# A constant for TensorE's idle matmuls, and a load of w1 split around a table: a fused spectral filter and Mish layer on one core

## The chip, the cores and the metric

The kernel runs on one core of a Trainium2 chip. The metric is the device time of one execution in microseconds. Three runs of the kernel before gave 135.14, 135.55 and 136.71 us, median 135.55.

## The reference

For x of 2048 x 512 (bf16) the reference mixes two branches by a gate for each row:

```
g = sigmoid((x * gate_w).sum(-1, keepdims=True))
a = irfft2(rfft2(x) * (w_r + 1j * w_i))          # spectral branch
h = x @ w1 + b1                                  # w1: 512 x 1792
b = (h * tanh(softplus(h))) @ w2                 # Mish, w2: 1792 x 512
out = g * a + (1 - g) * b
```

## The kernel before, in words

x is held as 16 tiles of 128 rows, in four chunks of four tiles. The spectral branch does both transforms as matmuls: TensorE transposes each x tile (`tr`, L516), VectorE forms sums and differences of the transposed tiles (L541, into Tg), TensorE multiplies these with a table FD (`a1`, L609 to L612) and then with matrices M1 (`s1`, L630); the result goes through a scratch tensor in HBM, is multiplied by the filter WT, and comes back by the inverse steps (L745, L798, L828, L846). The dense branch is layer 1 (`mm1`, L575: 14 column blocks of w1 for each chunk), Mish on ScalarE (L560), and layer 2 (L903).

The order of the work is not written out by hand. `_build` adds tasks with an engine, an estimated duration, a priority and their dependences to a graph; `schedule` walks through simulated time and lists the tasks of each engine: at each step it takes, of the tasks that could start within 0.1 us of the earliest, the one of highest priority. A load's estimated landing is when its turn on the DMA engines comes, plus its bytes over the `bw` entered for it, plus 0.6 us; a reader on another engine is due 0.05 us later. `run_engine` (L940) then issues each engine's list in that order, with semaphore waits where a dependence asks for one. So entered costs decide the order and nothing else; on the chip an engine waits in its list until the next task's inputs are there.

What the change touches lies in the head, the first ten or so microseconds:

- SyncE's queue issues the loads in the order of the code: the first half of x's chunk 0 (`ld_x0(0)`), row block 0 of w1's first 512 columns (`ld_w1d(0)`), the second half of the chunk (`ld_x0(1)`), the row blocks 1 to 3, the columns 512 to 1023 of w1 (`ld_w1(4, 8)`, 512 KB), the table FD (`ld_fd`, 192 KB), then chunk 1 of x, the rest of w1 (`ld_w1(8, 14)`), M1, chunks 2 and 3 of x, and small tables.
- GpSimd's queue holds the loads of the filter (WT) and of w2, which wait for the rest of w1.
- VectorE sets a tile zt of 128 x 256 to zero (L500). ScalarE applies Mish to one column of it (L501), which makes it load its function table. TensorE multiplies zt by itself (L504, the "idle" or filler matmuls): their results are not used. The planner puts such matmuls wherever TensorE has nothing else ready, until the first group of layer 1 is placed; at most 60 are offered, the first 15 of 256 columns, the rest of 128.
- Then come the small transpose of b1 (`tr_small`, L519), the transposes of the first half of the chunk, the first quarter of layer 1's first four column blocks on that half (`early0`, L590, which needs row block 0), the transposes of the second half, `early1` to `early3` (row blocks 1 to 3), and `late0` to `late3` (L590 too), the same four column blocks on the second half. Column block 4 (L575) follows, and the first `a1`, which needs FD.

L416 is the helper that issues every DMA, and L1017 the start of the program, where the engines meet and GpSimd writes a few built-in constants of one column.

Of the kernel before, what the change touches and what calls it, by code (L numbers as in the profile page):

```python
# [7 lines left out]
BF = mybir.dt.bfloat16  # L8
F32 = mybir.dt.float32
AF = mybir.ActivationFunctionType  # L10
# [20 lines left out]
def _bf16_bits(a):  # L31
    a = np.ascontiguousarray(a, dtype=np.float32)
    u = a.view(np.uint32)
    r = (u + np.uint32(0x7FFF) + ((u >> np.uint32(16)) & np.uint32(1))) >> np.uint32(16)
    return r.astype(np.uint16)
# [280 lines left out]
def _build(nc, A_x, A_w_r, A_w_i, B_x, B_w1, B_b1, B_w2, gate_w, out):  # L316
    cs = _build_consts()
    d_FD = nc.inline_tensor(_bf16_bits(cs["FD"]), name="c_fd").bitcast(BF)
# [7 lines left out]
    G = _Graph()  # L326
    es = ExitStack()
    with es:
        def sb(name, shape, dt):
            return es.enter_context(nc.sbuf_tensor(name, shape, dt))  # L330

        xo = sb("xo", [128, NT, 512], BF)
# [4 lines left out]
        act = sb("act", [128, 3, NFT, 512], BF)  # L337
        w1_sb = sb("w1_sb", [128, 4, F], BF)
        w2_sb = sb("w2_sb", [128, NFT, 512], BF)
        FDs = sb("FDs", [128, 768], BF)  # L340
# [6 lines left out]
        Ybuf = sb("Ybuf", [128, 32 * KR], BF)  # L347
        junk = sb("junk", [128, 512], BF)
        gwb = sb("gwb", [128, 512], BF)
        zt = sb("zt", [128, 256], BF)  # L350
        braw = sb("braw", [14, 128], BF)
        b1f = sb("b1f", [128, NFT], F32)
        gdot = sb("gdot", [128, NT], F32)
# [12 lines left out]
        q1 = sb("q1", [128, 2, 2, 16], F32)  # L366
# [25 lines left out]
        ps = es.enter_context(nc.psum_tensor("ps", [128, 8, 512], F32))  # L392
        psb = ps.bitcast(BF)

        xv = A_x[0].rearrange("(s p b) d -> p s b d", s=2, b=8)
        ov = out[0].rearrange("(s p b) d -> p s b d", s=2, b=8)
        w1v = B_w1.rearrange("(dt p) f -> p dt f", p=128)
# [7 lines left out]
        def new_sem(name):  # L405
            return es.enter_context(nc.semaphore(name))
# [5 lines left out]
        def dma(name, dst, src, reads=(), writes=(), nbytes=0, deps=(), is_out=False, prio=None, queue="sp", bw=300e3):  # L412
            dur = 1.0 if queue == "pool" else 0.5

            def fn(e, _dst=dst, _src=src):
                return e.dma_start(_dst, _src)  # L416

            t = G.add(name, queue, dur, fn, reads=reads, writes=writes, lat=2.0 + nbytes / bw, deps=deps, prio=prio)
            t.xfer = nbytes / bw
            t.isdma = True  # L420
            if is_out:
                t.sem = out_sem
                n_out_dma[0] += 1
                t.semval = 16 * n_out_dma[0]
            else:
                t.sem = new_sem("d_" + name)
                t.semval = 16
            return t
# [16 lines left out]
        def evict(name, n, dst, src, reads, writes, prio=None, rate=1.0):  # L445
# [9 lines left out]
              reads=["ones"], writes=["perm"])  # L455
        G.add("id14", "pool", 0.2, lambda e: e.affine_select(out=id14[:, :], in_=id14[:, :], pattern=[[1, 14]],
                                                             compare_op=ALU.is_equal, fill=0.0, base=0, channel_multiplier=-1),
              reads=["ones"], writes=["id14"])

        def ld_x(c, s0, s1):  # L460
            dma(f"ld_x{c}{s0}", xo[:, 4 * c + 2 * s0:4 * c + 2 * s1, :].rearrange("p (s b) d -> p s b d", b=2), xv[:, s0:s1, 2 * c:2 * c + 2, :],
                writes=[("x", t) for t in range(4 * c + 2 * s0, 4 * c + 2 * s1)], nbytes=128 * 2048 * (s1 - s0), bw=330e3 if c == 1 else 380e3)

        def ld_x0(b):
            dma(f"ld_x0{b}", xo[:, b:4:2, :], xv[:, :, b, :], writes=[("x", b), ("x", 2 + b)], nbytes=128 * 2048, bw=(218e3, 350e3)[b])

        def ld_w1d(dt_):
            dma(f"ld_w1d{dt_}", w1_sb[:, dt_, 0:512], w1v[:, dt_, 0:512], writes=[("w1d", dt_)], nbytes=128 * 1024, bw=350e3)

        def ld_w1(lo, hi):  # L470
            return dma(f"ld_w1_{lo}", w1_sb[:, :, 128 * lo:128 * hi], w1v[:, :, 128 * lo:128 * hi],
                       writes=[("w1", f) for f in range(lo, hi)], nbytes=512 * 256 * (hi - lo), bw=220e3 if lo == 4 else 380e3)

        dma("ld_b1", braw[:, :], B_b1.rearrange("(ft p) -> ft p", p=128), writes=["braw"], nbytes=3584, queue="act", prio=100.0)
        ld_x0(0)
        ld_w1d(0)
        ld_x0(1)
        for dt_ in range(1, 4):
            ld_w1d(dt_)
        ld_w1(4, 8)  # L480
        dma("ld_fd", FDs[:], d_FD[:], writes=["FD"], nbytes=128 * 1536, bw=262e3)
        ld_x(1, 0, 2)
        t_w1 = ld_w1(8, 14)
        dma("ld_m1", m1g1[:, 0:2048], d_M1.rearrange("p b h c m -> p (b h c m)"), writes=["m1"], nbytes=128 * 4096)
        ld_x(2, 0, 2)
# [4 lines left out]
        for i in range(2):  # L490
            for q in (0, 2, 1, 3):
                dma(f"ld_W{i}{q}", WT[32 * q:32 * q + 32, i, :, :].rearrange("p g k -> p (g k)"), Wv[i][q],
                    writes=[("W", i, q)], nbytes=32 * 8224, queue="pool", deps=[t_w1])
        WALL = [("W", i, q) for i in range(2) for q in range(4)]
        for h in range(2):
            dma(f"ld_w2_{h}", w2_sb[:, 7 * h:7 * (h + 1), :], w2v[:, 7 * h:7 * (h + 1), :],
                writes=[("w2", h)], nbytes=128 * 7 * 1024, queue="pool", deps=[t_w1])


        G.add("zero", "dve", 0.15, lambda e: e.memset(zt[:, :], 0.0), writes=["zt"], prio=99.0)  # L500
        G.add("table", "act", 1.5, lambda e: e.activation(q1[:, 0, 0, 0:1], zt[:, 0:1], AF.Mish), reads=["zt"], prio=99.0)  # L501
        for i in range(NWARM):
            n_ = 256 if i < 15 else 128
            G.add(f"warm{i}", "pe", n_ / 1200, lambda e, n_=n_: e.matmul(ps[:, 6, 0:n_], zt[:, 0:128], zt[:, 0:n_], start=True, stop=True),  # L504
               reads=["zt"], prio=1.0).filler = True


        SP0 = PR['sp0']
# [2 lines left out]
        def f_tr(e, ts, dts, at):  # L511
# [8 lines left out]
           reads=["braw", "id14"], writes=[("bank", 0)], prio=SP0 + 4.0)  # L520
        G.add("ev_small", "act", 0.25, lambda e: e.activation(b1f[:, :], psb[:, 0, 0:14], AF.Copy), reads=[("bank", 0)], writes=["b1f"], prio=SP0 + 1.05)
        for b in range(2):
            for dt_ in range(4):
                bk = (dt_ + 1) % 4
                pe(f"tr{b}d{dt_}", 2 * mm((256, 128)[b]), lambda e, dt_=dt_, bk=bk, b=b: f_tr(e, (b, 2 + b), (dt_,), lambda t, d_: (bk, t // 2)),
                   reads=[("x", b), ("x", 2 + b), "perm"], writes=[("bank", bk)], prio=SP0 + 1.0 + 2.5 * b - 0.01 * dt_)
# [3 lines left out]
                      reads=[("bank", bk)], writes=[("xT", t, dt_) for t in (b, 2 + b)], prio=SP0 + 1.1)  # L530

        for c in range(NCH):
            for t in range(4 * c, 4 * c + 4):
                if c > 0:
                    pe(f"tr{t}", 4 * mm(128), lambda e, t=t: f_tr(e, (t,), range(4), lambda t, dt_: (1, dt_)), reads=[("x", t), "perm"],
                       writes=[("bank", 1)], prio=SP0 + 1.0)
# [7 lines left out]
            for h, op in ((0, ALU.add), (1, ALU.subtract)):  # L544
# [3 lines left out]
                lo, hi = uv[:, 0:2, r2, :], uv[:, 2:4, r2, :]  # L548
# [45 lines left out]
        for dt_ in range(4):  # L594
            t_e = pe(f"early{dt_}", 4 * mm(256) * (1.8 if dt_ == 0 else 1), lambda e, dt_=dt_: f_early(e, range(4), (dt_,), 0), writes=[("bank", b) for b in EB],
                     reads=[("xT", 0, dt_), ("xT", 2, dt_), ("w1d", dt_)], prio=PR['mm1c0'] + 8)
            if dt_ == 0:
                G.filled = t_e
        for ft in range(4):
            pe(f"late{ft}", 4 * mm(256), lambda e, ft=ft: f_early(e, (ft,), range(4), 1), writes=[("bank", EB[ft])],  # L600
               reads=[("xT", t, dt_) for t in (1, 3) for dt_ in range(4)] + [("w1d", dt_) for dt_ in range(4)], prio=PR['mm1c0'] + 7 - 0.01 * ft)
            mish(0, ft, EB[ft])

        for t in range(NT):
            a1b = t % 2 if t >= 8 else 0

            def f_a1(e, t=t, a1b=a1b):
# [9 lines left out]
               writes=[("bank", a1b)], prio=SP0)  # L617
# [4 lines left out]
            if t % 4 == 3:  # L622
# [17 lines left out]
                for h in range(2):  # L640
                    t_r1w.append(dma(f"r1w{t}_{h}", scr1_w[h][:, b0:b0 + 8, :], Y1[64 * h:64 * h + 64, b0:b0 + 8, :],
                                     reads=[("Y1", b0 + i) for i in range(8)], writes=[("scr1", b0 + i, h) for i in range(8)],
                                     nbytes=64 * 8 * 512, prio=SP0 + 1.0, bw=180e3))
# [3 lines left out]
        for t in range(NT):  # L647
# [3 lines left out]
                  reads=[("x", t), "gw"], writes=[("gd", t), "junk"], deps=s1_tasks[2:3])  # L651
# [37 lines left out]
        for n in range(4):  # L689
            t_r1r.append(dma(f"r1r{n}", In2[:, :, 2 * n:2 * n + 2, :].rearrange("p q u k -> p q (u k)"), scr1_r[:, :, 512 * n:512 * n + 512],  # L690
                             reads=[("scr1", b, h) for b in range(32) for h in range(2)],
                             writes=[("In2", q, u) for q in range(4) for u in (2 * n, 2 * n + 1)],
# [43 lines left out]
        for n in range(4):  # L736
            zb = n % 2

            def f_s2(e, n=n):
                ins = None  # L740
                for c in range(2):
                    for q in range(4):
                        for h in range(2):
# [6 lines left out]
                               reads=[("In2", q, 2 * n + uu) for q in range(4) for uu in range(2)] + ["sm"], writes=BSB))  # L750
            for i in range(4):
                h, uu = divmod(i, 2)
                u, pb = 2 * (2 * n + uu) + h, uu
                for (nm, Pb, Wu) in (("1", P1b, WT[:, :, u, 0:256]), ("2", P2b, WT[:, ::-1, u, 0:256])):
# [5 lines left out]
                          reads=[("bank", 2 * h), ("bank", 2 * h + 1)] + WALL, writes=[("P" + nm, pb)])  # L760
                for (c, nm, Pb, op) in ((0, "1", P1b, ALU.subtract), (1, "2", P2b, ALU.add)):
# [3 lines left out]
                                reads=[("P" + nm, pb)], writes=[("Z", zb, i, c)])  # L765
                if n == 0 and i == 1:
                    s2_tasks.append(pe("s2x", 0.8, f_s2x, reads=[("In2", q, u_) for q in range(4) for u_ in range(8)] + ["sm", "rr"],
                                       writes=[("bank", 0), ("bank", 1)]))
# [4 lines left out]
                          reads=["q"], writes=["zr"])  # L773
                    G.add("zi", "pool", 0.15, lambda e: e.tensor_tensor(out=zi[:], in0=q2[:, 0], in1=q2[:, 1], op=ALU.add),
                          reads=["q"], writes=["zi"])
                    G.add("z0r", "pool", 0.15, lambda e: e.tensor_tensor(out=z0[:, 0, :], in0=zr[:, 0, :], in1=zi[:, 1, :], op=ALU.subtract),
                          reads=["zr", "zi"], writes=["z0r"])
                    G.add("z0i", "pool", 0.15, lambda e: e.tensor_tensor(out=z0[:, 1, :], in0=zi[:, 0, :], in1=zr[:, 1, :], op=ALU.add),
                          reads=["zr", "zi"], writes=["z0i"])
            if n == 0:  # L780
                G.add("gexp", "pool", 2.9, lambda e: e.tensor_tensor(out=gexp[:, :], in0=gbase[:, :], in1=gdot[:, :], op=ALU.pow),  # L781
                      reads=[("gd", t) for t in range(NT)] + ["gbase"], writes=["gexp"])
                G.add("gden", "pool", 0.2, lambda e: e.tensor_scalar(out=gexp[:, :], in0=gexp[:, :], scalar1=1.0, scalar2=None, op0=ALU.add),
                      reads=["gexp"], writes=["gden"])
                G.add("gcol", "dve", 0.2, lambda e: e.reciprocal(out=gcol[:, :], in_=gexp[:, :]), reads=["gden"], writes=["gcol"])
                G.add("omg", "dve", 0.1, lambda e: e.tensor_scalar(out=omg[:, :], in0=gcol[:, :], scalar1=-1.0, scalar2=1.0, op0=ALU.mult, op1=ALU.add),
                      reads=["gcol"], writes=["omg"])
            G.add(f"wc_{n}", "pool", 0.2, lambda e, n=n, zb=zb: e.tensor_copy(
                out=Zb[:, zb, :, :, :, 0], in_=z0[:].rearrange("p c (u h) -> p h c u", h=2)[:, :, :, 2 * n:2 * n + 2]),
                reads=["z0r", "z0i"], writes=[("Z", zb, 4)])  # L790

            def f_s2i(e, zb=zb):
# [10 lines left out]
               writes=BSB)  # L803
# [3 lines left out]
            for h in range(2):  # L807
                t_r2w.append(dma(f"r2w{n}{h}", scr2_w[h][:, :, 512 * n:512 * n + 512],
                                 T2s[64 * h:64 * h + 64, :, 2 * n:2 * n + 2, :].rearrange("p q u k -> p q (u k)"),
                                 reads=[("T2s", n, 0), ("T2s", n, 1)], writes=[("scr2", n, h)], nbytes=64 * 4096))  # L810
# [3 lines left out]
        for tq in range(8):  # L814
            b0 = 4 * tq
            dma(f"r2r{tq}", T2r[:, b0:b0 + 4, :], scr2_r[:, b0:b0 + 4, :],
                reads=[("scr2", n, h) for n in range(4) for h in range(2)], writes=[("T2r", b0 + i) for i in range(4)],
# [49 lines left out]
        for c in range(NCH):  # L867
# [7 lines left out]
            for tl in range(4):  # L875
                t = 4 * c + tl
                bank = 4 + (t % 2)
                if t == NT - 1:
                    G.cur_prio = PR['mm2'] - 10
                    for i, (c0, w_) in enumerate(((0, 384), (384, 128))):  # L880
                        cs_, bk = slice(c0, c0 + w_), 1 + i

                        def f_mm2h(e, t=t, tl=tl, bk=bk, hb=hb, cs_=cs_, w_=w_):
                            ins = None
                            for ft in range(NFT):
# [5 lines left out]
                           writes=[("bank", bk)])  # L891
# [3 lines left out]
                              reads=[("bank", bk), "omg", ("ga", t, 0), ("ga", t, 1), ("x", t)], writes=[("o", t, i)], prio=PR['fin'])  # L895
# [3 lines left out]
                for lo, hi in ((0, 4), (4, 7), (7, 11), (11, 14)):  # L899
                    def f_mm2(e, t=t, tl=tl, bank=bank, lo=lo, hi=hi, hb=hb):  # L900
# [7 lines left out]
                       reads=[("act", hb, ft) for ft in range(lo, hi)] + [("w2", lo // 7)], writes=[("bank", bank)])  # L908
                if t < NBF:
                    evict_b(t, bank)  # L910
                else:
# [3 lines left out]
                          reads=[("bank", bank), "omg", ("ga", t, 0), ("ga", t, 1)], writes=[("x", t), ("o", t)], prio=PR['fin'])  # L915
# [75 lines left out]
def bass_gated_mix__spectral_gfnet__dense_activation_mish__prompt_kernel(  # L991
    nc: bass.Bass,
    A_x: bass.AP,
    A_w_r: bass.AP,
    A_w_i: bass.AP,
    B_x: bass.AP,
    B_w1: bass.AP,
    B_b1: bass.AP,
    B_w2: bass.AP,
    gate_w: bass.AP,  # L1000
    out: bass.AP,
):
    _build(nc, A_x, A_w_r, A_w_i, B_x, B_w1, B_b1, B_w2, gate_w, out)
# [28 lines left out]
```

## Time and profile before

| | us |
|---|---|
| median of three runs | 135.55 |
| lowest, highest | 135.14, 136.71 |
| the profiled execution | 135.63 |
| its span, from the first to the last instruction | 133.9 |

The page gives busy time by engine (PE is TensorE's matmuls, PEld its loads of stationary operands, DVE VectorE, ACT ScalarE, POOL GpSimd, SP SyncE). The chain that ended last follows the work back from the last instruction, at each step to what released it; cut to a window and put in order of time, it reads as a list of what the kernel's end hung on. A group's line gives shortest, median and longest duration; a matmul's duration includes the time that it spends in the pipeline, so the rate is read from how many start in a stretch. A load's line gives its size and the time from issue to landing.

### The profile page before, as it was taken

What the parts mean: (1) busy time and instruction counts of PE and PEld (TensorE: products, weight loads), DVE (VectorE), ACT (ScalarE), POOL (GpSimd) and SP (SyncE); (2) the same over time, 40 slices, a digit from 0 to 9 for tenths busy, and PEclk for the clock granted to TensorE, in tenths of its full rate; (3) what the DMA queues carried; (4) which work ended last, traced back from release to release, by engine and by line L of the source; (5) the groups of instructions that cost most, each with busy time, mean ns of one, the idle gap of its engine ahead of it and who ended that gap; (6) DMA issues with size and microseconds to landing.
All of it is one profiled execution on the core that took longest, in us unless ns stands there. A gap on an engine that the chain in (4) does not pass through costs nothing.

```text
span 133.9 us, 2695 instructions
## 1 busy us (share of the span) xinstructions
PE 128.9 (96%) x1030; PEld 69.5 (52%) x1047; DVE 88.9 (66%) x213; ACT 79.6 (59%) x130; POOL 27.4 (20%) x56
## 2 busy tenths in 40 slices
PE   6999999999999999999999999999999999999992
PEld 4885655655544443443443443443445877755452
DVE  0286298989689982963893893794001699999422
ACT  4258798899988786605256657434333789792000
POOL 2000793014000009583440440440000000000000
PEclk9999999999999999999999999999999999999999
DMA  3899999999262399450600600600649700305321
GB/s 114 238 294 367 397 284 299 288 366 344 62 157 58 99 293 334 98 220 0 157 5 0 157 2 0 156 6 0 157 150 277 204 2 0 130 32 215 113 102 42
DMA packets 18937, 20.82 MB, mean 155 GB/s; under 512 B 1196, under 2 KB 16172, under 8 KB 18540
## 3 DMA queue, kind: packets, MB, share of 16 engines
q1 hardware_dynamic: 17888, 16.67, 41.1%
q0 software_dynamic: 864, 3.94, 9.4%
q8 instruction: 8, 0.13, 0.4%
q10 hardware_dynamic: 172, 0.04, 0.1%
q14 instruction: 5, 0.04, 0.1%
HBM read 14.35 MB, written 6.29 MB: 154 GB/s over the span
## 4 chain that ended last, share of the span: by engine, by line
PE 90%; ACT 6%; issue 1%; DVE 0%
PE ps L903 34%; PE ps L575 31%; PE ps L846 5%; ACT act L560 3%; PE ps L828 3%; ACT Ybuf L447 3%; PE ps L504 2%; PE ps L516 2%; PE ps L886 2%; PE ps L612 2%; PE ps L590 2%; PE ps L798 2%; PE ps L745 2%; PE ps L630 1%; PE ps L609 1%
## 5 line engine op out<-in xcount | busy, mean ns | idle before, releaser
L575 PE MATMUL ps<-xT,w_sb 128*128 128x512 bf16 x199 | 48.1, 379 | 0.8 <-issue 0.2
L903 PE MATMUL ps<-w_sb,act 128*128 128x512 bf16 x202 | 46.9, 379 | 0.6 <-issue 0.3
L560 ACT ACTIVATE act<-ps,b1f 128x512 bf16<-128x512 f32 x56 | 37.8, 692 | 12.8 <-PE ps L575 10.9
L903 PEld LDWEIGHTS ps<-w_sb,act 128*128 128x128 bf16 x210 | 20.2, 98 | 23.2 <-issue 1.2
L575 PEld LDWEIGHTS ps<-xT,w_sb 128*128 128x128 bf16 x208 | 19.4, 98 | 22.3 <-issue 2.1
L756 DVE TENSOR_TENSOR misc<-ps,WT 128x512 f32<-128x512 f32 x32 | 19.8, 681 | 5.9 <-PE ps L745 5.9
L858 ACT ACTIVATE xo<-ps,omg 128x512 bf16<-128x512 f32 x12 | 8.3, 690 | 19.5 <-PE ps L903 18.9
L762 POOL TENSOR_TENSOR misc<-misc 128x255 bf16<-128x255 f32 x17 | 12.1, 732 | 18.4 <-DVE misc L756 18.4
L446 DVE CAST Ybuf<-ps 128x512 bf16<-128x512 f32 (+1 forms) x9 | 8.2, 926 | 9.1 <-PE ps L798 7.3
L850 ACT ACTIVATE misc<-ps,gcol 128x512 f32<-128x512 f32 x16 | 10.7, 692 | 2.5 <-PE ps L846 2.4
L853 DVE TENSOR_TENSOR Tg<-misc 128x256 bf16<-128x256 f32 x32 | 11.7, 419 | 0.6 <-ACT misc L850 0.5
L446 DVE CAST misc<-ps 128x512 bf16<-128x512 f32 x7 | 4.8, 687 | 10.5 <-PE ps L828 10.5
L447 ACT ACTIVATE Ybuf<-ps 128x512 bf16<-128x512 f32 (+1 forms) x15 | 9.9, 714 | 2.9 <-PE ps L798 2.8
L649 DVE SCALAR_TENSOR_TENSOR junk<-xo,gwb 128x512 bf16<-128x512 bf16 x16 | 11.0, 690 | 0.7
L846 PE MATMUL ps<-GDs,misc 128*128 128x256 bf16 x64 | 9.3, 273 | 0.0
L447 ACT ACTIVATE Abuf<-ps 128x512 bf16<-128x512 f32 x13 | 7.7, 604 | 0.0
L446 DVE COPY xT<-ps 128x512 bf16<-128x512 bf16 x10 | 4.2, 422 | 4.6 <-PE ps L516 4.5
L516 PEld LDWEIGHTS ps<-pid,xo 128*128 128x128 bf16 x64 | 5.6, 111 | 3.1 <-DVE xT L446 0.4
L846 PEld LDWEIGHTS ps<-GDs,misc 128*128 128x128 bf16 x64 | 6.0, 98 | 2.1
L516 PE MATMUL ps<-pid,xo 128*128 128x128 bf16 x64 | 6.8, 243 | 0.0
L781 POOL TENSOR_TENSOR gexp<-gbase,gdot 128x16 f32<-128x16 f32 x1 | 2.9, 2943 | 18.5 <-DVE junk L649 18.5
L612 PE MATMUL ps<-FDs,Tg 128*128 128x256 bf16 x32 | 6.0, 273 | 0.0
(85 smaller groups left out, 112.8 us busy)
## 6 DMA issues: line engine op xcount, KB each, us to landing
scr<-Ybuf SPq DMA_DIRECT2D x16, 256.0 KB, 3.9
Abuf<-scr SPq DMA_DIRECT2D x4, 512.0 KB, 5.8
Abuf<-scr SPq DMA_DIRECT2D x8, 256.0 KB, 4.9
w_sb<-in_B_w_dram POOLq DMA_DIRECT2D x2, 896.0 KB, 14.2
out_dram<-xo SPq DMA_DIRECT2D x7, 256.0 KB, 2.1
xo<-in_A_x_dram SPq DMA_DIRECT2D x3, 512.0 KB, 9.8
WT<-in_A_w_r_dram POOLq DMA_DIRECT2D x4, 257.0 KB, 9.1
WT<-in_A_w_i_dram POOLq DMA_DIRECT2D x4, 257.0 KB, 10.8
```

The costliest lines, as they stand in the source:

```text
L446: G.add_multi(name, [("dve", dve_dur(n, rate=rate), lambda e: e.tensor_copy(out=dst, in_=src)), ("act", act_dur(n), lambda e: e.activation ...
L447: ("act", act_dur(n), lambda e: e.activation(dst, src, AF.Copy))],
L516: ins = e.transpose(psb[:, bank, 128 * col:128 * col + 128], xo[:, t, 128 * dt_:128 * (dt_ + 1)], perm[:, :])
L560: lambda e: e.activation(act[:, c % 3, ft, :].rearrange("p (t a b) -> p t a b", t=4, b=4), ps[:, bank, :].rearrange("p (t b a) -> p t a b" ...
L575: ins = e.matmul(ps[:, bank, :], w1_sb[:, dt_, 128 * ft:128 * (ft + 1)], xT[:, dt_, 4 * c:4 * c + 4, :], start=(dt_ == 0), stop=(dt_ == 3))
L649: lambda e, t=t: e.scalar_tensor_tensor(out=junk[:, :], in0=xo[:, t, :], scalar=1.0, in1=gwb[:, :], op0=ALU.mult, op1=ALU.mult, accum_out= ...
L756: lambda e, Pb=Pb, Wu=Wu, h=h, uu=uu, pb=pb: e.tensor_tensor(out=Pb[:, pb, :].rearrange("p (c j m) -> p c j m", c=2, j=2), in0=ps[:, 2 * h ...
L762: fz = (lambda e, c=c, Pb=Pb, op=op, pb=pb, h=h, uu=uu, zb=zb: e.tensor_tensor(out=Zb[:, zb, h, c, uu, 1:256], in0=Pb[:, pb, 1:256], in1=P ...
L846: ins = e.matmul(ps[:, yk, 256 * (j // 2):256 * (j // 2) + 256], TT[:, ts_, j // 2, s1, j % 2, :], GDs[:, j, :], start=(j % 2 == 0), stop= ...
L850: G.add(f"geo_{t}", "act", act_dur(512, True), lambda e: e.activation(gEO[:, gb, :], ps[:, yk, :], AF.Copy, scale=gcol[:, t:t + 1]), reads ...
L853: fg = (lambda e, i=i, op=op: e.tensor_tensor(out=ga[:, t, 256 * i:256 * i + 256], in0=gEO[:, gb, 0:256], in1=gEO[:, gb, 256:512], op=op))
L903: ins = e.matmul(ps[:, bank, :], act[:, hb, ft, 128 * tl:128 * (tl + 1)], w2_sb[:, ft, :], start=(ft == 0), stop=(ft == NFT - 1))
```

## The change

The idle matmuls read a built-in constant 1.0 of the library, one column wide and repeated by its access pattern, instead of the tile zt. The tile, its memset and the dependences on it go; the table's Mish reads the constant too. The first eight idle matmuls have 128 columns, the others 64, and the planner is told n / 600 us for n columns where it was told n / 1200. The load of w1's columns 512 to 1023 becomes two of 256 columns each, and the load of FD stands between them. The entered bandwidths of the head's loads change.

```diff
-        zt = sb("zt", [128, 256], BF)
...
         def ld_x0(b):
-            dma(f"ld_x0{b}", ..., nbytes=128 * 2048, bw=(218e3, 350e3)[b])
+            dma(f"ld_x0{b}", ..., nbytes=128 * 2048, bw=(403e3, 262e3)[b])
 
         def ld_w1d(dt_):
-            dma(f"ld_w1d{dt_}", ..., nbytes=128 * 1024, bw=350e3)
+            dma(f"ld_w1d{dt_}", ..., nbytes=128 * 1024, bw=(187e3, 238e3, 291e3, 187e3)[dt_])
 
         def ld_w1(lo, hi):
             return dma(f"ld_w1_{lo}", w1_sb[:, :, 128 * lo:128 * hi], w1v[:, :, 128 * lo:128 * hi],
-                       ..., bw=220e3 if lo == 4 else 380e3)
+                       ..., bw={4: 194e3, 6: 291e3}.get(lo, 380e3))
...
-        ld_w1(4, 8)
-        dma("ld_fd", FDs[:], d_FD[:], writes=["FD"], nbytes=128 * 1536, bw=262e3)
+        ld_w1(4, 6)
+        dma("ld_fd", FDs[:], d_FD[:], writes=["FD"], nbytes=128 * 1536, bw=115e3)
+        ld_w1(6, 8)
         ld_x(1, 0, 2)
...
-        G.add("zero", "dve", 0.15, lambda e: e.memset(zt[:, :], 0.0), writes=["zt"], prio=99.0)
-        G.add("table", "act", 1.5, lambda e: e.activation(q1[:, 0, 0, 0:1], zt[:, 0:1], AF.Mish), reads=["zt"], prio=99.0)
+        ones = nc.const_aps.tensor(1.0, (128, 256))
+        G.add("table", "act", 1.5, lambda e: e.activation(q1[:, 0, 0, 0:1], ones[:, 0:1], AF.Mish), prio=99.0)
         for i in range(NWARM):
-            n_ = 256 if i < 15 else 128
-            G.add(f"warm{i}", "pe", n_ / 1200, lambda e, n_=n_: e.matmul(ps[:, 6, 0:n_], zt[:, 0:128], zt[:, 0:n_], start=True, stop=True),
-               reads=["zt"], prio=1.0).filler = True
+            n_ = 128 if i < 8 else 64
+            G.add(f"warm{i}", "pe", n_ / 600, lambda e, n_=n_: e.matmul(ps[:, 6, 0:n_], ones[:, 0:128], ones[:, 0:n_], start=True, stop=True),
+                  prio=1.0).filler = True
```

More of the change, by code (lines that the diff above doesn't have):

```diff
@@ L464, in ld_x0 @@
         def ld_x0(b):
-            dma(f"ld_x0{b}", xo[:, b:4:2, :], xv[:, :, b, :], writes=[("x", b), ("x", 2 + b)], nbytes=128 * 2048, bw=(218e3, 350e3)[b])
+            dma(f"ld_x0{b}", xo[:, b:4:2, :], xv[:, :, b, :], writes=[("x", b), ("x", 2 + b)], nbytes=128 * 2048, bw=(403e3, 262e3)[b])
         def ld_w1d(dt_):
-            dma(f"ld_w1d{dt_}", w1_sb[:, dt_, 0:512], w1v[:, dt_, 0:512], writes=[("w1d", dt_)], nbytes=128 * 1024, bw=350e3)
+            dma(f"ld_w1d{dt_}", w1_sb[:, dt_, 0:512], w1v[:, dt_, 0:512], writes=[("w1d", dt_)], nbytes=128 * 1024, bw=(187e3, 238e3, 291e3, 187e3)[dt_])
         def ld_w1(lo, hi):
             return dma(f"ld_w1_{lo}", w1_sb[:, :, 128 * lo:128 * hi], w1v[:, :, 128 * lo:128 * hi],
-                       writes=[("w1", f) for f in range(lo, hi)], nbytes=512 * 256 * (hi - lo), bw=220e3 if lo == 4 else 380e3)
+                       writes=[("w1", f) for f in range(lo, hi)], nbytes=512 * 256 * (hi - lo), bw={4: 194e3, 6: 291e3}.get(lo, 380e3))
         dma("ld_b1", braw[:, :], B_b1.rearrange("(ft p) -> ft p", p=128), writes=["braw"], nbytes=3584, queue="act", prio=100.0)
```

## The prediction

> **What bounds the kernel now.** I read the page's busy shares first, then the chain that ended last, cut to the first 12 us (the stretch that the change touches), then the idle matmuls' own line, then each load's issue and landing.
>
> ```profile
> PE 128.9 (96%) x1030; PEld 69.5 (52%) x1047; DVE 88.9 (66%) x213; ACT 79.6 (59%) x130; POOL 27.4 (20%) x56
> ```
>
> TensorE is busy 128.9 of 133.9 us. Of the 5.0 us that it is not, 1.1 lie before its first matmul and 2.4 after its last (131.5 to 133.9), so 1.5 us are spread over all the rest. Whatever the head gains or loses shifts everything behind it.
>
> ```profile
> 0.89 0.18 DVE zt L500
> 1.07 0.05 issue
> 1.11 2.10 PE ps L504 x9
> 3.21 0.12 PE ps L519
> 3.33 1.18 PE ps L504 x5
> 4.51 0.85 PE ps L516 x8
> 5.37 0.85 PE ps L590 x4
> 6.22 0.85 PE ps L516 x8
> 7.07 1.89 PE ps L590 x16
> 8.97 0.02 issue
> 8.99 1.28 ACT act L560 x2
> 10.27 0.05 issue
> 10.31 0.81 PE ps L575 x3
> ```
>
> (start, length, what.) TensorE waits for VectorE to clear zt, then runs 14 idle matmuls (L504) around the small transpose of b1 (L519), then the first transposes of x (L516), layer 1's first quarter (L590, "early0"), eight more transposes, and the other 28 matmuls of L590; it is never without work. Until 7.07 us four 256-column matmuls take 0.85 us, 213 ns each; right after it sixteen take 1.89 us, 118 ns each. The array doubles its speed near 7.1 us, though the granted clock reads 1.00 in every slice. After 7.1 a 256-column matmul starts each 109 ns.
>
> ```profile
> L504 PE MATMUL ps<-zt x14: 393/421/421, 1.1 to 4.1; 128*128 128x256 bf16 x14
> ```
>
> The last of the idle matmuls starts at 4.1.
>
> ```profile
> xo<-in_A_x_dram SPq DMA_DIRECT2D x1, 256.0 KB, 2.7
> w_sb<-in_B_w_dram SPq DMA_DIRECT2D x1, 128.0 KB, 3.4
> xo<-in_A_x_dram SPq DMA_DIRECT2D x1, 256.0 KB, 3.6
> w_sb<-in_B_w_dram SPq DMA_DIRECT2D x1, 128.0 KB, 3.7
> w_sb<-in_B_w_dram SPq DMA_DIRECT2D x1, 128.0 KB, 4.3
> ```
>
> (The last column is us from issue to landing.) Issued at 0.80, 1.31, 1.81, 2.28 and 3.26, these land at 3.5 (x, first half), 4.7 (w1 row block 0), 5.4 (x, second half), 6.0 (block 1) and 7.5 (block 3). So x was there at 3.5 and its transposes began at 4.3: the idle matmuls overrun it by 0.8 us. But block 3, needed for early3, lands only at 7.5: no order of TensorE's work gets through L590 before 7.57 + 20 matmuls x 0.109 = 9.75. Now they end at 10.1. That bounds any gain here to about 0.35 us.
>
> **The change, part by part.** *The wait for zt goes.* The constant is written before the engines' common start, so TensorE begins when SP and POOL do, at 0.80 to 0.83 instead of 1.11: 0.28 us, all of it idle matmuls. VectorE's memset (0.17 us) and ScalarE's wait for it lie beside other work; ScalarE's table load begins at 1.5 after its own DMA issue: nothing.
>
> *How many idle matmuls.* The planner puts them in until the first transpose is due. Before: from 0.15 + 0.08 + 0.05 = 0.28 by 14 x 0.213 + 0.1 (b1) to 3.37, with x due at 1.512 + 1.203 + 0.65 = 3.365; 14 are in the trace. After: from 0, x due at 1.512 + 262144 B / 403 GB/s + 0.65 = 2.81; eight of 128 columns entered at 0.213 make 1.71, then four of 64 at 0.107, b1, and five more reach 2.80. So 8 + 9, 1600 columns.
>
> *What one costs.* Called without a type, the constant is float32, and no TensorE row here has an f32 operand. Below: as bf16, 128 columns in 107 ns (transposes, 0.85 / 8); 1600 columns in 1.33 us. On VectorE a multiplication over f32 takes 681 ns for 512 elements (L756), 1.33 ns each, a bf16 sum 0.69 us for 1024 (L541), 0.67 each: 4-byte data cost twice. A matmul has two f32 operands, streamed and stationary. Doubling once gives 213 ns per 128 columns, twice 427 (1600 columns: 2.67 or 5.33 us). I take the upper: both operands are of the kind that VectorE's row doubles for, and a product of two values split in halves has four parts. That is an estimate. By the Trainium skill, "FP8 and Floating Point Precision", section TensorE Precision Notes, true FP32 is four passes through the array; by it the sum would be the upper one, and no run here shows it yet.
>
> *The head's sum, in this execution.* The idle matmuls run 0.83 + 5.33 + 0.12 (b1) = 6.3, where the transposes began at 4.3. From there to the end of L590 are 10240 columns (16 transposes of 128, 32 matmuls of 256). Before: 4.31 to 7.1 slow, 3350 columns; 6890 remain, at 0.109 us per 256 2.93, end 10.0 (trace 10.1). After: 6.3 to 7.1 slow, 924; 9316 remain, 3.97, end 11.07. All landings but the last are past by then. So +1.0 us, if the speed doubles at 7.1 again. If it doubles at 5.0, before is held by block 3 at 9.75 and after ends at 10.05 by the same count: +0.3; at 6.0, +0.8; at 4.3, 0. I take the middle, +0.65 us. The doubling's moment is not set by the kernel alone: by the Trainium skill, "TensorE: Matmul & The Clock Gate", Part 1, a free-running window of about 3.4 us must have been busy; the trace's 7.1, 6.0 us after the first matmul, fits that and shows only one phase.
>
> *The piece of w1 in two, the table between.* One more issue on SP: 0.43 to 0.50 us (the loads' rows), so all later loads issue about 0.45 later. The rows of 1024 bytes become 512: in the packet records 46 ns and 27 ns, so 512 x 46 / 16 engines = 1.47 us become 1024 x 27 / 16 = 1.73, 0.26 more. The loads behind are stretched out by the DMA engines, not the issue (landing times grow from 5.8 to 13.5 us), so 0.26 to 0.45 us. Behind it on SP: x of chunk 1 lands at 11.8, used at 12.16; the next piece of w1 lands at 14.0, used at 15.5; the matrix M1 at 15.3, used at 16.7. With TensorE 0.65 to 1.0 later all are covered; without that cover x could be late by 0.45 - 0.36 = 0.1 us. POOL's queue waits for that next piece too (12.7 us, its longest wait) before it loads W and w2, which are first used at 52 and 55: covered by tens of us. The table FD would land some 0.9 earlier (256 KB less before it) than 10.06; its first reader stands at 10.96 behind a layer-1 group: no gain. The second half of the piece lands near 10.4, its first reader is at 12.7 (L575's third group). Zero.
>
> *The planner's new costs.* The entered times of the loads change, and with them perhaps the order of later work. The bounds: the 1.5 us of idle in between could shrink (0 to -0.5, since most of it is many pieces of 0.05), or one more wait for an eviction could open, at most a mish row of 0.69 us. I take 0, since both engines' queues have ready layer-1 work to the 57th us.
>
> Sum: 135.63 (this execution: 133.9 span and 1.7 around it, 0.08 above the median 135.55) + 1.0 in its own phase; against the median +0.65: **136.2 us**.
>
> **The rivals.** *Faster: an f32 column costs at most twice a bf16 one.* Then the idle matmuls end at 0.83 + 2.67 + 0.12 = 3.6, just as x lands; the transposes end at 4.5, early0 waits for block 0 (4.7), and the end of L590 is 9.82 in this phase, 9.75 in an early one: 0 to -0.35, less 0.1 for x of chunk 1. 135.4 us, and as low as 134.9 if the blocks land some tenths earlier. It decides below 300 ns per 128 columns: there 1600 columns take 3.75 us, the transposes start at 4.7 and about meet block 0. For it: the planner's entry of 213 ns is what a bf16 256-column matmul takes, but it is an entry, not a row. Against: the two doublings.
>
> *Much slower: the weights are no longer loaded beside the matmul before.* Now a load of zt takes 151 ns under a 213 ns matmul. Four passes with one load of 151 ns left uncovered per matmul make 578 ns of the 427 and 364 of the 213: 6.3 us at the slow rate are past after 8 wide and 4 narrow ones, the rest run at double speed to about 8.0, and L590 ends at 8.0 + 4.37 = 12.4, +2.3: 137.9 us. It passes 1% from half of that load on. For it: a load of another kind of operand is in no row. Against: layer 1's loads all hide.
>
> *The planner's order opens or closes a wait:* -0.5 to +0.7 on any of these, 135.0 to 136.9. The chain is TensorE for 90% and its pieces follow each other, which speaks for something to lose; little is to be won.
>
> *The change does not do what it says:* if the doubling of the clock comes a window earlier because matmuls start 0.28 us earlier, after's idle matmuls would shorten themselves and L590 end at 9.75: -0.35, 135.2. It is part of the faster case.
>
> **How the numbers follow.** Forecast (four times the bf16 rate) 0.54; faster rival with the early clock 0.28; uncovered weight loads 0.10; order alone 0.08. About 1% (1.36 us) is what a measurement of this kernel can tell from no change. Slower by over 1%, above 136.9: the uncovered loads, 0.10, and about 0.08 of the forecast (+1.0 with a new wait or a late clock). Faster by over 1%, below 134.2: only several gains together, 0.04. Within: 0.78. The range takes in the faster rival's 134.9 and the forecast's late phase with some of a new wait, 137.2; it leaves out most of the uncovered loads and a little below. The forecast's own range is 135.5 to 136.9.
>
> **What would show it.** Right: 17 idle matmuls from about 0.83, the wide ones starting each 427 ns or two passes of 213; first transposes near 6.3 (earlier if the clock doubles before); L590 ending at 10.1 to 11.1, and no load that TensorE waits for. Wrong: transposes at 3.6 with waits for the blocks of w1 behind them (faster rival); idle matmuls ending past 7 (weights uncovered); or a head as forecast and a total elsewhere, with a TensorE gap past 12 us that before has not (order).

## The result, and the profile after

| | before | after |
|---|---|---|
| median, us (six runs each) | 135.56 | 137.52 |
| profiled execution | 135.63 | 137.42 |
| its span | 133.9 | 135.7 |

The ratio of after to before is 1.0123, 95% interval 1.0074 to 1.0172 (one run of after, 140.76 us, is disturbed and not in it). The kernel became slower by about 1.9 us (2.0 between the medians, 1.7 by the ratio); the prediction said 136.2 and at most 137.2.

The page's busy shares, then the chain up to the first L609 (start, length, what), of the changed kernel:

```profile
PE 132.3 (98%) x1067; PEld 72.4 (53%) x1067; DVE 90.1 (66%) x214; ACT 78.5 (58%) x128; POOL 26.8 (20%) x56
```

```profile
0.83 5.14 PE ps L504 x24
5.98 0.11 PE ps L519
6.09 1.26 PE ps L504 x10
7.35 0.13 PE ps L516 x2
7.47 0.02 issue
7.50 0.30 DVE xT L529
7.80 0.05 issue
7.84 0.61 PE ps L590 x4
8.46 0.45 PE ps L516 x8
8.90 3.06 PE ps L590 x28
11.96 0.86 PE ps L575 x4
12.82 0.06 PE ps L609
```

TensorE is busier and later. The idle matmuls (L504) fill the time from 0.83 to 7.35. They are 34 records for 17 matmuls: an f32 matmul stands as two records, here called its passes. The first full group of layer 1 (L575) ends at 12.82; in the profile before it ended at 11.13, where the first L609 begins. From there to the span's end it is 135.7 - 12.82 = 122.9 us, before 133.9 - 11.13 = 122.8. So of the 1.8 us between the two spans the head has 1.7; what lies behind took as long as before, though the planner's order behind the head changed.

The idle matmuls by form (busy time, mean of one in ns), and their weight loads between 4.4 and 5.3 us, when the narrow ones ran at the slow pace:

```profile
L504 PE MATMUL ps<-const-float32-1.0 128*128 128x128 f32 x16 | 3.8, 429 | 0.8 <-PEq L1017 0.8
L504 PE MATMUL ps<-const-float32-1.0 128*128 128x64 f32 x18 | 2.9, 322 | 0.0
```

```profile
L504 PEld LDWEIGHTS ps<-const-float32-1.0 128*128 128x128 f32 x6 | 1.4, 333 | 0.0
```

The 16 wide passes take 0.83 to 4.38, 213 ns each by their starts (4.38 to 4.17, 4.17 to 3.95): 427 ns a matmul, as forecast. The 18 narrow ones stream half the columns and should have taken half; at the slow pace they start each 213 ns too, and each 112 ns once the speed has doubled (near 5.6 us here). From 4.4 to 5.34 us the row above has six loads (one of them began before), and in the trace they start each 213 ns. The records for a load (333 ns) overlap, so it is the spacing that tells.

Of the loads, the table FD landed 4.21 + 4.5 = 8.7 where it landed at 10.1; its first reader, which moved with everything else, stood at 12.66. Nothing waited for it in either kernel.

### The profile page after: what moved, and what is told of

Same layout as the page of the kernel before. It is cut to its first block, busy times and chain, and to the rows that moved or that the text cites. A ratio compares the mean times of both kernels' runs of the same rounds, so it can differ in the third digit from the quotient of the medians.

```text
span 135.7 us, 2753 instructions
## 1 busy us (share of the span) xinstructions
PE 132.3 (98%) x1067; PEld 72.4 (53%) x1067; DVE 90.1 (66%) x214; ACT 78.5 (58%) x128; POOL 26.8 (20%) x56
## 4 chain that ended last, share of the span: by engine, by line
PE 95%; ACT 3%; DVE 0%; issue 0%
PE ps L903 34%; PE ps L575 33%; PE ps L846 5%; PE ps L504 5%; PE ps L590 3%; PE ps L828 3%; PE ps L886 2%; PE ps L612 2%; PE ps L516 2%; PE ps L798 2%; PE ps L745 2%; PE ps L630 1%; ACT Ybuf L446 1%; ACT act L560 1%; PE ps L609 1%; PE ps L610 1%
## 5 line engine op out<-in xcount | busy, mean ns | idle before, releaser
L575 PE MATMUL ps<-xT,w_sb 128*128 128x512 bf16 x208 | 49.7, 379 | 0.1
L903 PE MATMUL ps<-w_sb,act 128*128 128x512 bf16 x210 | 48.6, 379 | 0.0
L560 ACT ACTIVATE act<-ps,b1f 128x512 bf16<-128x512 f32 x56 | 37.9, 692 | 12.6 <-PE ps L575 10.7
L575 PEld LDWEIGHTS ps<-xT,w_sb 128*128 128x128 bf16 x208 | 19.2, 98 | 22.1 <-ACT act L560 2.2
L445 DVE CAST misc<-ps 128x512 bf16<-128x512 f32 x8 | 5.4, 685 | 10.3 <-PE ps L828 10.3
L504 PE MATMUL ps<-const-float32-1.0 128*128 128x64 f32 (+1 forms) x34 | 6.5, 373 | 0.8 <-PEq L1017 0.8
L446 ACT ACTIVATE Abuf<-ps 128x512 bf16<-128x512 f32 x12 | 7.1, 605 | 0.0
L504 PEld LDWEIGHTS ps<-const-float32-1.0 128*128 128x128 f32 x34 | 6.2, 284 | 0.8 <-issue 0.8
L529 DVE COPY xT<-ps 128x256 bf16<-128x256 bf16 x4 | 1.0, 292 | 8.1 <-PE ps L516 8.1
```

The costliest lines, as they stand in the source:

```text
L445: G.add_multi(name, [("dve", dve_dur(n, rate=rate), lambda e: e.tensor_copy(out=dst, in_=src)), ("act", act_dur(n), lambda e: e.activation ...
L446: ("act", act_dur(n), lambda e: e.activation(dst, src, AF.Copy))],
L504: G.add(f"warm{i}", "pe", n_ / 600, lambda e, n_=n_: e.matmul(ps[:, 6, 0:n_], ones[:, 0:128], ones[:, 0:n_], start=True, stop=True), prio= ...
L560: lambda e: e.activation(act[:, c % 3, ft, :].rearrange("p (t a b) -> p t a b", t=4, b=4), ps[:, bank, :].rearrange("p (t b a) -> p t a b" ...
L575: ins = e.matmul(ps[:, bank, :], w1_sb[:, dt_, 128 * ft:128 * (ft + 1)], xT[:, dt_, 4 * c:4 * c + 4, :], start=(dt_ == 0), stop=(dt_ == 3))
L903: ins = e.matmul(ps[:, bank, :], act[:, hb, ft, 128 * tl:128 * (tl + 1)], w2_sb[:, ft, :], start=(ft == 0), stop=(ft == NFT - 1))
```

## The experiments

The versions up to the eleven idle matmuls keep, unless the text says otherwise, the changed kernel's loads, entered costs and order on all engines; only what the diff shows differs. Times are medians, ratios are to the kernel before run beside them on the same chip.

Theory: all of the loss is the price of the idle matmuls; a narrow f32 one costs as much as a wide one, because loading its stationary operand sets the pace. Rivals: the split load and the new order cost part of it; or an f32 pass has a floor whatever its operands.

**Are the narrow ones bound by their weights?** Two versions: the stationary operand halved, and the streamed one doubled.

```diff
-            G.add(..., lambda e, n_=n_: e.matmul(ps[:, 6, 0:n_], ones[:, 0:128], ones[:, 0:n_], start=True, stop=True),
+            G.add(..., lambda e, n_=n_: e.matmul(ps[0:64, 6, 0:n_], ones[:, 0:64], ones[:, 0:n_], start=True, stop=True),
```

> The changed kernel, f32 kept, but the idle matmuls' stationary operand has 64 columns instead of 128; same number, same places. Theory (a narrow f32 pass of 64 streamed columns is bound by loading its 128 stationary columns, 213 ns at the slow rate): the narrow ones go from two passes of 213 ns to two of about 107, the wide ones stay at 427; the transposes begin about 1 us earlier than in the changed kernel (near 6.2 instead of 7.2), 136.4 to 136.9 us. Rival (an f32 pass has a floor of 213 ns, whatever its weights): narrow ones unchanged, 137.5 us.

Measured: 136.44 us, ratio 1.0067 (1.0038 to 1.0096), 0.56% below the changed kernel's ratio and in the range of the theory. The two ratios' intervals overlap a little, so the spacing of the matmuls tells more than the time. The narrow ones in the window where all ran at the doubled speed, the weights of 64 columns here and, below, of 128 in the changed kernel:

```profile
5.06:5.47 0.41, 0.41 (x9) 0.41 (x9) 1.00 1.08 250
```

```profile
6.29:7.07 0.78, 0.78 (x9) 0.78 (x9) 1.00 0.95 284
```

(window, its length, TensorE's busy time and records in it, its loads', granted clock, DMA share, GB/s; a record that reaches into the window counts.) The starts are 58 ns apart with 64 stationary columns and 112 ns with 128: half the weights, half the time, the streamed columns unchanged. The floor per pass is out. With 64 stationary columns the result has 64 rows instead of 128 too; but 128 rows of result alone do not set the pace, since the narrow bf16 matmuls of the version with the bf16 constant (below) write 128 and start each 53 ns at the slow pace. The slow pace of narrow ones with 64 was not seen, since the speed doubled at 4.2 in this execution.

```diff
-            n_ = 128 if i < 8 else 64
-            G.add(f"warm{i}", "pe", n_ / 600, ...
+            n_ = 128
+            G.add(f"warm{i}", "pe", (0.2 if i < 8 else 0.1) * 16 / 15, ...
```

(The new expression enters the same durations as before, so that number and order stay.)

> The changed kernel with the nine narrow f32 idle matmuls widened from 64 to 128 streamed columns, number and places kept. Theory (loading the 128 f32 stationary columns sets a narrow one's pace): a wide one starts each 213 ns a pass too, so nothing changes, 137.5 us within 0.4. Rival (the price goes by streamed columns, as forecast, and the narrow ones were slow for another reason): nine times 0.11 to 0.21 us more, 138.5 to 139.4.

Measured: 137.44 us, ratio 1.0130 (1.0096 to 1.0164), the changed kernel's 1.0123 again. The widened ones, at the slow pace and at the doubled one:

```profile
4.38:5.34 0.96, 0.96 (x6) 0.96 (x6) 1.00 0.84 258
6.90:7.69 0.79, 0.79 (x9) 0.79 (x8) 1.00 0.77 233
```

In windows of the same length the changed kernel's narrow ones have as many records: six at the slow pace, nine at the doubled one. (In this execution the idle matmuls end at 7.8 instead of 7.2, because the speed doubled near 6.8 instead of 5.6.) Nine matmuls with twice the streamed columns cost nothing that the interval tells, where the rival asked for 1.0 us or more: the price by columns is refuted. Together with the halved weights this shows that the load sets the pace.

**Is anything lost beside the idle matmuls?** Fewer of them, f32 kept; then the cleared tile of before in their place.

```diff
-            n_ = 128 if i < 8 else 64
-            G.add(f"warm{i}", "pe", n_ / 600, ...
+            n_ = 128
+            G.add(f"warm{i}", "pe", 0.45, ...
```

> The changed kernel with the f32 constant kept, but six idle matmuls of 128 columns (five, b1, one) instead of 17, all the rest in the same order. Theory: 6 x 427 ns from 0.83 and b1 end at 3.5, just as x lands; layer 1's first blocks end near 9.8; 135.2 to 135.6 us. Rival (split and order): 136.2 or more.

Measured: 135.11 us, ratio 0.9972 (0.9956 to 0.9987), about 2.0 us below the changed kernel by the ratios, and a little under the range expected.

> The changed kernel's loads, entered costs and order, but the idle matmuls of the kernel before (bf16, the tile zt that VectorE clears, 256 columns): eleven by the planner's new due time. Theory: 1.11 + 11 x 0.213 + 0.12 = 3.6, as x lands; 135.2 to 135.6 us, the same as with the bf16 constant within 0.3. Rival (split and order): 136.2 or more. If the 0.28 us earlier start of the constant's matmuls matters for the doubling of the speed, this one is later by some tenths than the six wide ones.

Measured: 135.28 us, ratio 0.9979 (0.9961 to 0.9997). In both the loads are split and the order is the new one, and both are faster than before: split and order cost nothing that shows. (Their heads are earlier than that of the kernel before, which could hide a small cost; but the same eleven cleared matmuls with the old loads, below, have a ratio of 0.9992, so with like heads the split load is not the slower one.) The 0.28 us of the earlier start made no difference between them that these intervals tell.

**The constant alone,** on the kernel before (its loads, costs and order; the planner then puts in 8 wide and 14 narrow).

> The kernel before, loads and order unchanged, with only the f32 constant and the new idle matmuls: 8 wide and 14 narrow by the planner, five more than in the changed kernel. Theory (the loss lies in the idle matmuls alone): the changed kernel's 137.5 and five times 0.22 (fast) to 0.43 us (slow) more, 138.4 to 139.4. Rival (split and order carry part of the loss): 137.5 or less.

Measured: 138.03 us, ratio 1.0157 (1.0127 to 1.0187). The idle matmuls alone bring a loss of at least the changed kernel's size. With five more of them 138.4 us or more was expected, which is missed; the interval overlaps the changed kernel's, so what the five cost is not settled. The profiled execution took 141.59 us, and in it the speed doubled only near 12.9 us. Its narrow ones behind b1, in the chain:

```profile
6.31 4.46 PE ps L504 x20
```

All twenty passes ran at the slow pace, and in the trace they start each 213 ns. Why the speed doubled so late here is not shown.

**The constant in bf16,** first with the narrow forms, then with 256 columns.

```diff
-        ones = nc.const_aps.tensor(1.0, (128, 256))
+        ones = nc.const_aps.tensor(1.0, (128, 256), BF)
```

> The changed kernel with the built-in constant in bf16 instead of f32; the same 17 idle matmuls in the same places, every other engine's order as in the changed kernel. Theory (all of the loss is the price of f32 in the idle matmuls): the wide ones start each 107 ns, the narrow ones at most as long, they are past by about 2.5 us, the first transposes begin when x lands (3.5 to 3.8), layer 1's first blocks end near 9.8, and the time is 135.2 to 135.6 us, 1.9 below the changed kernel. Rival (the split load and the new order cost part of it): 136.2 us or more, with the head as said.

Measured: 135.89 us, ratio 1.0028 (1.0008 to 1.0047). Neither range was met. The head as its timeline shows it (start, length, engine, what, and in brackets the idle time before):

```profile
0.84 1.23 PE L504 MATMUL ps<-const-bfloat16-1.0 128*128 128x128 bf16 x12 [0.84 <-PEq L1017]
2.71 0.19 PE L519 MATMUL ps<-pid,braw 14*128 14x14 bf16 x1 [0.65 <-DMA braw<-in_B_b_dram]
2.83 0.45 PE L504 MATMUL ps<-const-bfloat16-1.0 128*128 128x64 bf16 x5
3.56 1.03 PE L516 MATMUL ps<-pid,xo 128*128 128x128 bf16 x8 [0.28 <-DMA xo<-in_A_x_dram]
4.45 1.01 PE L590 MATMUL ps<-xT,w_sb 128*128 128x256 bf16 x4
5.41 1.03 PE L516 MATMUL ps<-pid,xo 128*128 128x128 bf16 x8
6.23 4.62 PE L590 MATMUL ps<-xT,w_sb 128*128 128x256 bf16 x28
10.69 1.03 PE L575 MATMUL ps<-xT,w_sb 128*128 128x512 bf16 x4
```

The idle matmuls are now so cheap that TensorE waits 0.65 us for b1 and 0.28 for x, and 28 matmuls of L590 take 4.62 us where after's take 3.22: they run at the slow pace until about 9 us. x came in time, the speed did not. This execution took 136.34 us, 0.45 above the median, and the shortest of the twelve 135.11, so the late doubling is seen in one trace, and how late it comes in the others is not known. The next version keeps TensorE busy until x lands:

```diff
-            n_ = 128 if i < 8 else 64
-            G.add(f"warm{i}", "pe", n_ / 600, ...
+            n_ = 256
+            G.add(f"warm{i}", "pe", n_ / 1200, ...
```

> The changed kernel with the bf16 constant and idle matmuls of 256 columns, thirteen by the planner (ten, b1, three), all other work in the changed kernel's order. Theory (what counts is that TensorE is kept busy from 0.83 until x lands and no longer): 0.83 + 13 x 0.213 + 0.12 = 3.7, no idle stretch as with the short bf16 ones, so the speed doubles by 5 to 7.5; 134.9 to 135.3 us. Rival (the bf16 constant itself, or the loads, cost something): 135.6 to 135.9, as with the short bf16 matmuls.

Measured: 135.00 us, ratio 0.9956 (0.9938 to 0.9974), the fastest; run once more beside another version (below) 135.14, ratio 0.9981 (0.9971 to 0.9991). It is faster than both kernels.

```profile
0.83 2.29 PE ps L504 x10
3.12 0.17 PE ps L519
3.29 0.75 PE ps L504 x3
4.04 0.85 PE ps L516 x8
4.90 0.67 PE ps L590 x4
5.56 0.45 PE ps L516 x8
6.01 3.06 PE ps L590 x28
```

(the chain) L590 begins its 28 at 6.01 instead of 8.90, at full speed. Between this version and the short bf16 one the idle matmuls are all that differs, and the time by 0.9 us; that it is the clock rests on the two traces.

**What does an early head gain with the old loads?** The kernel before with eleven idle matmuls (`NWARM = 11`), and with the thirteen of the fastest version.

> The kernel before with eleven idle matmuls instead of fourteen, nothing else. Theory (the 0.2 to 0.4 us won by the versions whose idle matmuls end as x lands come from that alone): transposes at 3.6 to 3.9 instead of 4.3; 135.1 to 135.3 us against 135.5. Rival (they come from the split load and its order): 135.5, no change.

Measured: 135.48 us, ratio 0.9992 (0.9974 to 1.0010): no gain; the rival held. The timeline shows why in this execution, which took 135.89 us, 0.4 above the median:

```profile
10.97 1.03 PE L575 MATMUL ps<-xT,w_sb 128*128 128x512 bf16 x4
12.47 0.40 PE L516 MATMUL ps<-pid,xo 128*128 128x128 bf16 x4 [0.48 <-DMA xo<-in_A_x_dram]
```

TensorE has caught up with x of chunk 1, which lands at 12.4, and gives back 0.5 us.

> The kernel before, its loads, entered costs and order unchanged, with thirteen bf16 idle matmuls of 256 columns on the built-in constant (ten, b1, three), so that the head is the same as in the version with the changed kernel's loads. Theory (with an early head the old loads make TensorE wait for x of chunk 1, 0.5 us in the version with eleven idle matmuls, and the split load with its order is what spares it): 135.3 to 135.6 us, 0.2 to 0.5 above that version. Rival (the earlier start of the idle matmuls by 0.28 us made the difference): 135.0, the same as that version.

> The bf16 constant, thirteen idle matmuls of 256 columns, and the changed kernel's loads and order, once more beside the same work with the old loads. Theory and rival alike: 134.9 to 135.2 us; what counts is the distance to the other.

Measured: old loads 135.55 us, ratio 1.0006 (0.9985 to 1.0026); new loads and order 135.14, ratio 0.9981 (0.9971 to 0.9991). With the same head the split load, the table's place and the order that goes with them are worth 0.4 us, the size that the theory gave. Its mechanism is not borne out: the trace with the old loads shows the wait for x of chunk 1 at 0.15 us only. In these two traces the 0.4 us stands already where the first L575 begins, 9.81 against 9.38: the speed doubled at 6.3 against 5.9, and the last row block of w1, issued before the split load, landed at 7.6 against 7.1 and cost a wait of 0.22. Where the edit gains is open. One thing the timelines do show: x of chunk 1 lands no earlier with the new loads (12.3 and 12.6 in the two executions with thirteen bf16 matmuls, 12.1 and 12.4 with the old loads). What keeps TensorE from waiting for it is the new order, which puts three column blocks of layer 1 (L575) ahead of the transposes of chunk 1 where the old order has two.

## Why the prediction was wrong, point by point

- *What bounds the kernel:* right for the loss: the head's 1.7 us arrived at the end undiminished. A gain is not kept whole: in the fastest version's trace the first L609 starts 1.2 us earlier than before (9.77 against 10.96), and the span is 0.8 shorter (133.1 against 133.9).
- *The wait for zt goes:* right, 0.83 instead of 1.11.
- *How many idle matmuls:* right, 8 + 9.
- *What one costs:* this step failed, by a size. The row-based estimate of four times bf16 holds for the wide ones, 427 ns. By the Trainium skill, "FP8 and Floating Point Precision", section TensorE Precision Notes, true FP32 takes four passes through the array; that agrees in price, while the profile shows two records of twice the time each. For the narrow ones the prediction put 213 ns, by columns streamed; it is 427 at the slow pace and 224 at the fast one, since their two loads of 128 f32 columns set it. At one pace throughout, that is 9 x 0.213 = 1.9 us left out; here, where the speed doubled at 5.6, the idle matmuls ended 0.9 us later than forecast (7.2 instead of 6.3) in spite of it.
- *The head's sum:* in the same way. For a doubling between 5.0 and 6.0 it gave +0.3 to +0.8; the trace has +1.7. The same sum with the doubling at 5.6 ends the idle matmuls near 6.0 and L590 near 10.4 (an estimate); the trace has 7.2 and 11.8. So 1.2 us come from the idle matmuls. The other 0.2 it left out: early0 waits for its transposed x, since transposes at full speed end before VectorE's copy (the chain's 0.30 of L529). (From 6.3 to 7.1 at the slow pace are some 960 columns and not 924, which moves its end by less than 0.05.)
- *The rival of uncovered weight loads:* its mechanism was near, with 0.10 the chance given. It expected a bf16 load's 151 ns in addition to the passes for every matmul; the loads turned out to hide under the wide passes and to replace the narrow ones' time. Its sign, idle matmuls that end past 7, came. Its 137.9 was nearer to 137.52 than the forecast, in part by luck: its wide ones were too dear (578 ns for 427) and its narrow ones too cheap (364 for 427).
- *The faster rival:* refuted as to f32's price. But its time, 135.4 and as low as 134.9, is about what the versions with idle matmuls that end as x lands show with the new loads: 135.0 to 135.3. The bound of 0.35 us on any gain was one execution's landing and no bound: row block 3 landed at 7.5 there, at 6.3 in the fastest version's trace, whose L590 ended at 8.9 instead of 9.75.
- *The split load:* "zero" holds in the changed kernel, where TensorE is late: x of chunk 1 landed at 12.2, 0.4 later than before, in the range given. Without that cover the fastest version's trace has a wait for x of about 0.1 us, the size forecast, and the other early heads with the split load none. The prediction did not see that the old loads with an early head wait too, 0.15 and 0.5 us.
- *The order:* taken as 0, and in the changed kernel it was, 122.8 us before against 122.9 after behind the head.
- *The range:* it ended at 137.2 since the late phase was priced with cheap narrow matmuls; 137.52 lies past it. The 1% named as the least that can be told was too coarse: the versions with nine or more executions have intervals of 0.1 to 0.2% to either side.

## What to carry to other kernels

Before a cheap filler is given a price by the columns that it streams, look at its other operand: a matmul also loads its stationary operand, 128 columns here, and with f32 that load is what a short one waits for. Work that only fills a wait must end when the awaited load lands, neither later nor earlier: here 17 f32 fillers cost 1.9 us, and 17 bf16 ones that ended too soon left the kernel 0.4 slower than before, in the trace at hand by a late clock. A gain in the head is kept only if the next load is early too, or other ready work stands ahead of it in the order; see what TensorE waits for next.

## What the runs showed of the hardware

An f32 matmul is two records; with 128 x 128 operands each takes 213 ns before the speed doubles and 112 after it. An f32 load of 128 stationary columns paces short passes at 213 ns, and at 112 at double speed, where 64 stationary columns give 58. In bf16 the load of 128 columns does not show: narrow matmuls of 64 streamed columns start each 53 ns at the slow pace.

The matmuls all began between 0.83 and 1.12, but the moment of doubling was 7.1 us before, 5.6 after, from 4.2 to 7.1 in most other versions, 9.0 in the head with short bf16 matmuls, which idles 0.65 us for b1, and 12.9 in the profiled execution of the constant alone, which has no such wait. The profile's granted clock read 1.00 from the start in all of them. By the Trainium skill, "TensorE: Matmul & The Clock Gate", Part 1, the gate opens after a busy window of about 3.4 us, and the window is free-running. By an estimate from that figure a doubling comes at most two windows, 6.8 us, after steady work begins. In most traces it came 3.3 to 6.0 us after the first matmul, and with the short bf16 ones 5.5 after the last of the idle stretches, which agrees; the 12.1 us of the constant alone do not, and no run here shows why.
